# Column-group passes over 32 of a segment's 40 rows for Q and K in a recurrent forward stage, with row-major bf16 stores behind it

## The chip, the cores and the metric

One core of one Trainium2 chip. The metric is the device time of one execution in microseconds (us). Each kernel was executed several times, in rounds with the kernel before on the same chip. The jobs ran on different chips, on which the kernel before took medians of 3449 to 3478 us; kernels of different jobs are therefore compared by their ratios to it, or by stages.

## The reference, cut to what matters

A transformer layer with a recurrent memory, forward and all gradients. The sequence of 2048 tokens is cut into 64 segments of 32. Each segment attends over 40 rows: 8 memory rows and its own 32. The output of the 8 memory rows is the memory of the next segment, so the 64 segments depend on each other. A gated feed-forward block (FFN) follows.

```python
D, H, Dh = 448, 16, 256            # so H*Dh = 4096
M, seg, S, F = 8, 32, 2048, 1792
mem = mem0
for s in range(64):
    h = concat([mem, layernorm(x)[s*32:(s+1)*32]])     # 40 x 448
    q, k, v = h @ Wq, h @ Wk, h @ Wv                   # 40 x 16 x 256 each
    p = softmax(where(mask, q k^T * Dh**-0.5, -1e9))
    o = (p v) @ Wo                                     # 40 x 448
    mem = o[:8];  outs.append(o[8:])
h  = x + concat(outs)
h2 = h + (silu(n(h) @ w_gate) * (n(h) @ w_up)) @ w_down   # n = layernorm
# outputs: h2 and the gradients of x, mem0, Wq, Wk, Wv, Wo, w_gate, w_up, w_down
```

## The kernel before

The program has five stages, one after the other: start-up, the forward recurrence, the FFN (forward and backward of the block), the backward recurrence and the weight gradients (below: the tail). These are the parts that the change and the argument touch. `P` is 128, `KC` is 4 (448 rows in four chunks of 128), `MC` is 32 (4096 columns in chunks of 128), `L` is 40, `cj` is a permutation of the 32 chunks.

```python
# forward, per segment
def wpass(W_sb, s, dst):                       # called for Q and for K: 128 matmuls each
    for j in range(MC):
        c = cj(j); b, jj = divmod(j, 12)
        for kc in range(KC):                   # stationary 128x128 weights, 40 columns stream
            nc.tensor.matmul(pss[b][:, jj*L:(jj+1)*L], lhsT=W_sb[:, kc, c*P:(c+1)*P],
                             rhs=hT_roll[:, kc, sl, :], ...)
    ...                                        # three evacuations to dst, feature-major
# [...]
wpass(Wq_sb, s, qT);  wpass(Wk_sb, s, kT)
# scores: 32 matmuls, stationary 128x64; then V: 32 matmuls, stationary 128x64, 512 columns stream
# [...] softmax of all 8 head pairs, P transposed, 16 matmuls P V -> three PSUM banks
for j in range(MC):                            # memory rows only, through Wo
    nc.tensor.matmul(pO[32*(j%4):32*(j%4)+M, 0:D], lhsT=o8[:, j, :], rhs=Wo_sb[:, cj(j), :], ...)
# [...]
if r == 3:                                     # every 4th segment: 128 own rows through Wo
    for j in range(MC):
        nc.tensor.matmul(px[:, 0:D], lhsT=xblk[:, j, :], rhs=Wo_sb[:, cj(j), :], ...)
    to_token_major(xblk, t)                    # DMA transpose, then 128 x 2048 rows into X_o[t]
# [...] Q and K of the segment are stored feature-major (QT, KT); the backward reads them
#       with one DMA transpose each per segment

# tail, output-projection gradient: 20 row tiles, two halves
def load_x(nm, hf):
    for t in (range(NT) if nm != "o" else order):
        x_t = ring()
        src = dr["X_" + nm][t][:, hf*2048:(hf+1)*2048]      # 128 partitions x 4 KB
        if nm == "o": nc.sync.dma_start(out=x_t, in_=src)
        # [...]
dcs = dr["DHb"].rearrange("(t p) d -> p t d", p=P)[:, :, 0:D]
for t0, t1 in ((0, 4), (4, NT), (NT+1, NB), (NT, NT+1)):    # DHb in four loads
    nc.gpsimd.dma_start(out=DCt[:, t0:t1], in_=dcs[:, t0:t1])
xo = load_x("o", 0)
# six accumulators first: every one of them needs all 20 tiles
rows_by_d(...)
```

## Time and profile before

| stage, from the first and last matmuls of each | us |
|---|---|
| start to the first scores of segment 0 | 75.3 |
| forward, per segment (63 periods) | 17.506 |
| last scores to the first FFN matmul | 75.8 |
| FFN and the set-up of the backward | 367.5 |
| backward recurrence | 1131.3 |
| tail, of it the output-projection part | 711.4, 141.2 |

The median is 3460.1 us (3452.44 to 3460.38, 3 runs). A stage is read as the time between two marks in the trace, each of them the first or last matmul of a certain line. The times of the table all stand on one clock, so only their differences are used.

From the page of the kernel before: totals, three strips of 40 time slices (tenths of busy time, of the granted clock, and of the DMA engines' busy time), and four groups of matmuls (line, engine, operation, names, shapes, count, then busy us and mean ns of one, then idle before them). A copy of a finished PSUM bank to SBUF is called its evacuation; feature-major means features along the partitions, row-major (or token-major) means rows along them. In the names arA, arB and arW are SBUF areas, psf, po, fx and ph are PSUM banks; X_o (after: Os and Or) are the head outputs in DRAM, DHb is the gradient of the rows behind the attention, M_v and X_v are parts of the gradient of V.

```profile
span 3461.7 us, 120955 instructions
...
PE 3042.7 (88%) x55028; PEld 2056.9 (59%) x55038; DVE 1321.4 (38%) x2921; ACT 974.9 (28%) x2181; POOL 620.8 (18%) x1304
...
PE   3999999999999658892999999989999898999999
...
PEclk8999999999999879996999999999999999999999
DMA  7344633543534797799687878787887988888661
...
L360 PE MATMUL psf<-arA,arW 128*128 128x40 bf16 x16384 | 433.6, 181 | 62.0 <-POOL arA L345 35.8
...
L399 PE MATMUL psf<-arW,arA 128*64 128x512 bf16 x2048 | 259.5, 382 | 0.0
...
L462 PE MATMUL fx<-arW,arA 128*128 128x448 bf16 x512 | 124.5, 353 | 0.0
L437 PE MATMUL po<-arW,arB 128*8 128x448 bf16 x2048 | 110.7, 359 | 3.7
...
```

TensorE is busy nearly all the time in the forward stage (slices 2 to 13), at full clock; DMA engines are on average under half busy. The largest group, L360, is `wpass`.

The chain of waits of the kernel before in the forward stage (100 to 1160 us), as shares by engine and line:

```profile
...
by line: PE psf L360 38.2%; PE psf L399 18.4%; PE po L437 9.9%; PE fx L462 9.2%; PE psf L446 4.9%; PE psf L391 3.9%; issue 3.0%; DVE arB L75 2.9%; PE psf L420 2.2%; PE psf L428 1.8%; ACT arB L77 1.2%; DVE om L442 0.6%; DVE arA L449 0.6%; DV
...
```

Nearly all of the chain is TensorE work: Q and K 38%, V (L399) 18%.

The same kernel in windows; the columns are the window, its length, the busy time of five engines with the number of instructions, the granted clock, the DMA share and GB/s:

```profile
...
core 0: us, PE busy (x) PEld busy (x) DVE busy (x) ACT busy (x) POOL busy (x), PEclk, DMA share, GB/s
100.00:1160.00 1060.00, 996.90 (x24443) 772.84 (x24432) 449.03 (x1023) 334.78 (x733) 158.89 (x368) 0.99 0.44 139
1700.00:2700.00 1000.00, 932.77 (x21552) 659.09 (x21553) 461.02 (x1171) 374.89 (x970) 209.56 (x474) 0.98 0.79 165
2745.00:2785.00 40.00, 34.62 (x216) 15.60 (x209) 6.36 (x14) 3.29 (x7) 7.24 (x11) 0.87 1.03 381
...
```

The second row is the backward recurrence, with DMA busy for 0.79; the third is the head of the tail.

One forward segment of the kernel before in the timeline of TensorE (start us, length us, what, how many):

```profile
...
start us, us, engine line op out<-in xcount [idle before <-releaser]
...
500.61 6.56 PE L360 MATMUL psf<-arA,arW 128*128 128x40 bf16 x256
507.10 0.56 PE L391 MATMUL psf<-arA 128*64 128x40 bf16 x24
...
507.90 3.62 PE L399 MATMUL psf<-arW,arA 128*64 128x512 bf16 x30
511.54 0.38 PE L420 MATMUL psf<-ident,arB 128*40 128x40 bf16 x16
...
513.79 1.69 PE L437 MATMUL po<-arW,arB 128*8 128x448 bf16 x32
...
```

Long runs of one kind: 256 matmuls with a stationary operand of 128 columns, then scores and V with 64.

### The profile page before, as it was taken

The numbers are of one execution on the slowest core, as the hardware profiler recorded it, in microseconds if no ns is written. First come the engines' busy times: TensorE is split into PE (matmuls) and PEld (weight loads), VectorE is DVE, ScalarE is ACT, GpSimd is POOL, SyncE is SP. The second block draws the span as 40 slices with busy tenths as digits, with TensorE's granted clock in tenths as the row PEclk, the third lists the DMA queues.
The fourth block names the chain that finished last, engine by engine and source line by source line (L and its number), as shares of the span: only waits on it lengthen the run. The fifth ranks groups of instructions, "written<-read, shape, count | busy, mean of one in ns | idle before, by whom it ended". The sixth has DMA issues, their size and how long they took to land.

```text
span 3461.7 us, 120955 instructions
## 1 busy us (share of the span) xinstructions
PE 3042.7 (88%) x55028; PEld 2056.9 (59%) x55038; DVE 1321.4 (38%) x2921; ACT 974.9 (28%) x2181; POOL 620.8 (18%) x1304
## 2 busy tenths in 40 slices
PE   3999999999999658892999999989999898999999
PEld 2777777777777446661666666666666544444444
DVE  4444444444444246771444444444444301111111
ACT  1333333333333223330333333333333202111100
POOL 3111111111111111111112211211221211111121
PEclk8999999999999879996999999999999999999999
DMA  7344633543534797799687878787887988888661
GB/s 264 132 130 133 174 127 130 162 146 127 156 130 147 134 210 182 178 212 239 139 164 167 174 161 165 166 160 163 172 167 162 275 241 185 174 176 179 160 247 38
DMA packets 997173, 583.91 MB, mean 169 GB/s; under 512 B 906100, under 2 KB 916420, under 8 KB 995060
## 3 DMA queue, kind: packets, MB, share of 16 engines
q1 hardware_dynamic: 926788, 340.27, 47.5%
q0 software_dynamic: 67568, 233.95, 19.8%
q8 instruction: 430, 7.05, 0.9%
q10 hardware_dynamic: 2304, 1.97, 0.2%
q14 instruction: 83, 0.68, 0.1%
HBM read 104.05 MB, written 250.19 MB: 102 GB/s over the span
## 4 chain that ended last, share of the span: by engine, by line
PE 61%; issue 13%; DMA 9%; DVE 8%; SPq 4%; ACT 2%; POOL 2%; ACTq 0%; DVEq 0%; POOLq 0%
PE psf L360 12%; PE po L756 8%; PE psf L399 6%; PE psf L713 5%; PE psf L691 4%; PE po L437 3%; PE fx L462 3%; PE fx L815 3%; PE psf L536 2%; PE psf L921 2%; PE psf L942 2%; PE psf L778 2%; DVE arA L75 2%; PE psf L446 2%; PE fx L602 2%
## 5 line engine op out<-in xcount | busy, mean ns | idle before, releaser
L77 ACT CAST arA<-psf 128x320 bf16<-128x320 f32 (+4 forms) x1139 | 487.9, 447 | 1595.2 <-PE psf L360 422.0
L75 DVE CAST arA<-psf 128x384 bf16<-128x384 f32 (+6 forms) x1029 | 492.5, 496 | 1075.9 <-PE psf L921 359.9
L360 PE MATMUL psf<-arA,arW 128*128 128x40 bf16 x16384 | 433.6, 181 | 62.0 <-POOL arA L345 35.8
L360 PEld LDWEIGHTS <-arW 128*128 128x128 bf16 x16384 | 432.2, 97 | 76.5 <-issue 57.3
L756 PE MATMUL po<-arW,arA 128*32 128x448 bf16 x6144 | 359.2, 365 | 40.5 <-DVE arA L75 21.0
L713 PE MATMUL psf<-arA,arW 128*128 128x40 bf16 x8192 | 219.2, 180 | 55.5 <-POOL arA L648 44.8
L921 PE MATMUL psf<-arW,arA 128*128 128x512 bf16 x990 | 250.7, 381 | 10.3 <-DMA arW<-X_k 5.3
L713 PEld LDWEIGHTS <-arW 128*128 128x128 bf16 x8192 | 214.9, 96 | 75.2 <-issue 74.8
L399 PE MATMUL psf<-arW,arA 128*64 128x512 bf16 x2048 | 259.5, 382 | 0.0
L756 PEld LDWEIGHTS <-arA 128*32 128x32 bf16 x6144 | 156.3, 98 | 160.7 <-issue 32.9
L536 PE MATMUL psf<-arA,arW 128*128 128x256 bf16 x1344 | 163.8, 283 | 94.4 <-DMA arA<-arA 68.7
L921 PEld LDWEIGHTS <-arA 128*128 128x128 bf16 x1440 | 135.2, 98 | 184.7 <-issue 39.2
L536 PEld LDWEIGHTS <-arW 128*128 128x128 bf16 x1344 | 136.3, 102 | 124.3 <-issue 100.4
L399 PEld LDWEIGHTS <-arA 128*64 128x64 bf16 x2048 | 147.3, 111 | 66.5 <-issue 0.2
L75 DVE CAST arB<-psf 40x320 bf16<-40x320 f32 x320 | 108.0, 337 | 98.1 <-PE psf L428 64.7
L77 ACT CAST arB<-psf 128x96 bf16<-128x96 f32 (+1 forms) x320 | 98.3, 307 | 103.5 <-DVE arB L75 51.0
L691 PEld LDWEIGHTS <-arW 128*128 128x128 bf16 x2048 | 88.4, 101 | 65.7 <-issue 62.1
L723 ACT COPY arA<-psf 128x1024 bf16<-128x1024 bf16 x128 | 123.3, 1015 | 4.7 <-PE psf L722 3.1
L462 PE MATMUL fx<-arW,arA 128*128 128x448 bf16 x512 | 124.5, 353 | 0.0
L437 PE MATMUL po<-arW,arB 128*8 128x448 bf16 x2048 | 110.7, 359 | 3.7
L691 PE MATMUL psf<-arB,arW 128*128 128x80 bf16 x2048 | 99.1, 203 | 16.7 <-DVE arB L740 7.7
L942 PE MATMUL psf<-arW 128*128 128x448 bf16 x450 | 95.4, 361 | 5.4 <-DMA arW<-X_o 5.3
(461 smaller groups left out, 3760.6 us busy)
## 6 DMA issues: line engine op xcount, KB each, us to landing
QT<-arA POOLq DMA_DIRECT2D x64, 512.0 KB, 4.0
KT<-arA SPq DMA_DIRECT2D x64, 512.0 KB, 3.5
VG<-arA SPq DMA_DIRECT2D x64, 512.0 KB, 3.1
X_o<-arA POOLq DMA_DIRECT2D x40, 512.0 KB, 4.5
X_v<-arA POOLq DMA_DIRECT2D x32, 512.0 KB, 6.2
X_k<-arA POOLq DMA_DIRECT2D x32, 512.0 KB, 4.2
X_q<-arA POOLq DMA_DIRECT2D x32, 512.0 KB, 4.2
arW<-X_o SPq DMA_DIRECT2D x30, 512.0 KB, 13.9
```

The costliest lines, as they stand in the source:

```text
L75: nc.vector.tensor_copy(out=out, in_=in_)
L77: nc.scalar.copy(out=out, in_=in_)
L360: nc.tensor.matmul(pss[b][:, jj * L:(jj + 1) * L], lhsT=W_sb[:, kc, c * P:(c + 1) * P], rhs=hT_roll[:, kc, sl, :], start=(kc == 0), stop=( ...
L399: nc.tensor.matmul(pV[b][64 * g:64 * g + 64, 0:512], lhsT=hT_flat[:, kc, sl * L:sl * L + 64], rhs=Wv_sb[:, kc, n * 512:(n + 1) * 512], sta ...
L437: nc.tensor.matmul(pO[32 * (j % 4):32 * (j % 4) + M, 0:D], lhsT=o8[:, j, :], rhs=Wo_sb[:, cj(j), :], start=(j < 4), stop=(j >= MC - 4), sk ...
L462: nc.tensor.matmul(px[:, 0:D], lhsT=xblk[:, j, :], rhs=Wo_sb[:, cj(j), :], start=(j == 0), stop=(j == MC - 1))
L536: nc.tensor.matmul(ps[:, f2 * 256:(f2 + 1) * 256], lhsT=Wt[:, kc, c * P:(c + 1) * P], rhs=xT[:, kc, :], start=(kc == 0), stop=(kc == KC - 1))
L691: nc.tensor.matmul(ps[b][:, i * 2 * L:(i + 1) * 2 * L], lhsT=lhs[:, cl, :], rhs=rhs_bd[:, cl // 2, :, :].rearrange("p g n -> p (g n)"), st ...
L713: nc.tensor.matmul(pss[b][:, jj * L:(jj + 1) * L], lhsT=WoT_sb[:, kc, c * P:(c + 1) * P], rhs=do_roll[:, kc, sl, :], start=(kc == 0), stop ...
L756: nc.tensor.matmul(pH[32 * (j % 4):32 * (j % 4) + 32, 0:D], lhsT=blk[nm][:, j, r * SEG:(r + 1) * SEG], rhs=WT[:, cj(j), :], start=(nm == " ...
L921: nc.tensor.matmul(pa[2 * kc + g][:, 0:w], lhsT=lhs_of(b)[:, kc * P:(kc + 1) * P], rhs=rhs_of(b, g), start=(b == 0), stop=(b == nblk - 1), ...
L942: nc.tensor.matmul(pa[i][:, 0:D], lhsT=lhs_of(b, i), rhs=rhs_of(b), start=(bi == 0), stop=(bi == len(nblk) - 1))
```

## The change

The intent: stream the weights instead of the 40 rows. A segment's 40 rows are its 32 own ones and 8 of memory. In the forward, Q and K of 32 of them, the last 24 own rows and the 8 memory rows, come from matmuls with 32 stationary columns and 512 streaming ones; four of them share the array, one in each group of 32 columns (`quad(q)` is the q-th block of 32 output partitions). Q and K of the first 8 own rows, which don't depend on the memory, are made in advance for four segments together ("rest"). What the backward reads of Q, K and the head outputs is stored row-major in bf16, so that it gets Q and K with plain loads. The output projection takes the same 32 rows at once; the extra projection of 128 rows every fourth segment becomes one every sixteenth, for the first 8 own rows of 16 segments.

```diff
+def col_pass(k, ps, W_sb, rows, b):
+    Wv = W_sb.rearrange("p c (g h d n) -> p c g h d n", g=2, h=8, d=2)
+    for kc in range(k.KC):
+        for q in range(4):
+            k.nc.tensor.matmul(ps[quad(q), 0:512], lhsT=rows(kc), rhs=Wv[:, kc, q % 2, 4*b:4*b+4, q // 2, :], ...)
 # per segment
-wpass(Wq_sb, s, qT);  wpass(Wk_sb, s, kT)
-# scores, V, softmax, P, values, one after the other over all heads
+proj(Wk_sb, 0, Kst, "s"); proj(Wq_sb, 0, Qst, "v")     # a proj is a col_pass and its evacuation
+to_features(0)                                         # 8 transposes, one copy
+pS0 = scores(0)
+proj(Wk_sb, 1, Kst, "s"); proj(Wq_sb, 1, Qst, "v")
+softmax(0, pS0)
+to_features(1); pS1 = scores(1)
+for b in range(4): value_rows(b)
+transposed_p(0); softmax(1, pS1); values(0); out_proj(0)
+transposed_p(1); values(1); out_proj(1)
# [... rest(t + 1) every fourth segment; oT, residual, stores of mean and variance to MV ...]
 # stage of the head outputs
-to_token_major(xblk, t)                                # X_o[t]: 128 tokens x 4096
+nc.gpsimd.dma_start(out=dr["Os"][s], in_=stg)          # Os[s]: (d g i) = 128 rows x 1024
 # backward, per segment
-nc.sync.dma_start_transpose(out=Q_sb, in_=dr["QT"][s])
-nc.sync.dma_start_transpose(out=K_sb, in_=dr["KT"][s])
+# [... four plain loads each for Q and K, rows of 2 KB ...]
 # tail
-                nc.sync.dma_start(out=x_t, in_=src)
+                src = dr["Os"][4*t:4*t+4].rearrange("r (d g i) c -> d g r i c", d=2, g=2)
+                for g in range(2):
+                    nc.sync.dma_start(out=x_t[:, g*1024:(g+1)*1024], in_=src[hf, g])
-    # DHb in four loads
+    # DHb in 20 loads, into 8, 24 or 128 partitions each [...]
```

## The prediction

> **What bounds the kernel now.** Table of stages: forward recurrence 83–1175 us, PE busy 94%, clock 0.98, DMA 44%; boundary 1175–1243, PE nearly idle; FFN to 1581; backward set-up to 1644; backward recurrence to 2745, PE 92%, DMA 79%; weight gradients to 3462, PE about 95%. Forward is 64 dependent segments of about 17.0 us, and the chain of waits there is mostly PE: Q/K passes 38%, V 18%, output projection 10%, row residual (fx) 9%, issue 3%. Undisturbed backward segments take 16.04 us, the average is 17.2: about 75 us of stalls over the stage ("issue", DH loads).
>
> **Costs, from trace durations.**
> - Q/K: 256 matmuls of 40 columns take 6.56 us a segment. Afterwards 64 matmuls of 32x512 in four column groups. The four-column-group matmuls of 448 columns in the backward (43 in 2.2 us) run 45 ns apart, so about 53 ns each: 3.4 us. The Trainium skill (TensorE: Matmul & The Clock Gate, Part 3) says column tiles run concurrently; this trace agrees (45 ns against 183 ns alone).
> - Added: 16 transposes (0.97 us in the backward); their two evacuations on DVE at 0.69 us each (128x1024 bf16 from PSUM); mask matmuls 0.15 us.
> - Output projection stays at about 1.7 us; V at 3.5 us.
> - Residual: 32 matmuls per 4 segments (1.55 us a segment) become 0.45 us; but Q/K of memory rows' counterparts ("rest") add about 1.1 us.
> - PE per segment: about 15.9 -> 13.9 us.
> - Chain: K0/Q0, evacuation, transposes, evacuation, scores, softmax in halves, ... , values, projection, one copy of 256 columns instead of two of 224. Adding measured durations gives 14.2–15 us; DVE rises from about 7.2 to 10 us a segment and sits on the chain, so it may queue. V fills the softmax gaps.
> So I expect 15.0 us a segment (14.4 to 16.2), on the critical path nearly in full: 64 x 2.0 = -128 us.
>
> - Backward: two of three DMA transposes a segment become plain 2 KB-row loads, and stores halve. DMA share falls from 0.79 to 0.4–0.5. Q/K loads are off the chain; only the stalls can shrink: -30 us (0 to -60).
> - Boundary: tiny-element load of mean/variance before the FFN, +5 us. Start-up ("rest" of tile 0, more set-up), +4 us.
> - Tail: each 512 KB o tile becomes two loads whose source has an outermost dimension of 4. The Trainium skill (DMA: Bandwidth & Descriptors, "Why a DMA increments its semaphore by 16") says the outermost sizes of both sides fix how many of 16 engines work; that would be 4. No run here shows it. If so, the first weight gradient, already waiting for o tiles (2760–2783), loses perhaps 50 us; even odds: +25 us.
>
> **Prediction.** Sum about -125 us: 3335 us, 80% range 3250 to 3425. Faster by over 2%: 0.76; within 2%: 0.20; slower: 0.04.
>
> **What would show it.** Column passes about 53–55 ns apart, 16 per 0.9 us. Segment period near 15 us; if it is over 16, the chain should show DVE (feature copies, softmax halves) and PE idle above 10%. Backward DMA share below 0.5, average segment under 17 us. PE waits "DMA <- Os" in the tail, and the time to landing of Os loads well above the old 9–14 us, if four engines carry them. No change in FFN body.
>
> **What would make it wrong.** The static instruction order may put evacuations or POOL copies of the memory rows behind late work, or make PE wait for half-softmax twice, lengthening the chain to 17 us; the "rest" work may not fit the gaps; the o loads may cost more than 50 us. On the good side, the chain may drop to the PE sum (13.9 us) and the backward stalls vanish: near 3230 us.

## More of the kernel before

The queue of SyncE in the tail of the kernel before:

```profile
...
2746.41 35.24 SPq L884 DMA_DIRECT2D arW<-X_o  x20
...
```

The queue issues twenty loads of 512 KB in 35.24 us, so 1.76 us each.

## The result, and the profile after

After: 3599.02 us median (3588.35 to 3610.84, 4 runs). Before, in the same rounds: 3460.24 us (3452.44 to 3461.64, 4 runs). The ratio is 1.0396 (95% interval 1.0358 to 1.0433), so the change made the kernel 4% slower; the results are correct. A ratio here is the mean time of one kernel's runs over that of the other's of the same rounds, so not quite the ratio of the medians.

| stage | before | after | difference | predicted |
|---|---|---|---|---|
| start to first scores | 75.3 | 88.5 | +13.2 | +4 |
| forward, 63 periods | 17.506 each | 17.391 each | -7 | -128 |
| last scores to FFN | 75.8 | 88.4 | +12.6 | +5 |
| FFN and set-up | 367.5 | 367.9 | 0 | 0 |
| backward | 1131.3 | 1092.2 | -39 | -30 |
| tail | 711.4 | 866.9 | +155.5 | +25 |
| of it output-projection part | 141.2 | 275.5 | +134.3 | |

The differences sum to +135 us. Two lines make the error: the forward gained almost nothing, and the tail lost six times what was allowed for. Two cautions: the forward is measured here from the first score to the last, over 63; from the start of one segment's scores to the start of the next it is 17.493 and 17.331 us, so -10 us in place of -7. And the stretch from last scores to FFN took 56.6 and 71.7 us in two other kernels with the code of before in this place (before_sw128, before_sw32), so single profiles don't settle its +12.6.

From the page of the kernel after, the answers to the lines of before:

```profile
span 3601.2 us, 106692 instructions
...
PE 3038.5 (84%) x46908; PEld 1831.5 (51%) x46918; DVE 1403.6 (39%) x3384; ACT 1023.4 (28%) x2404; POOL 847.7 (24%) x1789
...
PE   3999999999998188874999999999993198899998
...
PEclk9999999999999699987999999999997599999999
DMA  7334444533533968799555655545556358788661
...
L286 PE MATMUL psf<-arW,arA 128*32 128x512 bf16 x4096 | 302.3, 393 | 46.2 <-POOL arA L387 37.4
L500 PE MATMUL psf<-arW,arA 128*64 128x512 bf16 x2048 | 269.1, 382 | 0.0
...
L492 PE MATMUL po<-arW,arA 128*32 128x192 bf16 (+1 forms) x4096 | 135.9, 260 | 17.1 <-DVE arA L75 17.1
...
L1069 PE MATMUL fx<-arW 128*128 128x448 bf16 x30 | 11.0, 387 | 130.1 <-DMA arW<-Or 116.1
...
```

There is a hole of two slices in the strip of TensorE near the start of the tail; in the second of them the DMA share is 0.3 and the clock 0.5. L286 are the column passes: 302.3 us in place of the 433.6 us of L360 (its matmuls for rest, into fx, not counted). This "busy" counts overlapping matmuls once, and it leaves out the time between two matmuls, which is where the forward's loss turned out to be. L1069 is the output-projection part: TensorE stood idle for 130.1 us in front of its matmuls into fx, all but 14 us of it ended by a load of Or.

The chain of waits after, in the same forward window:

```profile
...
by line: PE psf L286 25.5%; PE psf L500 22.1%; PE po L492 11.4%; PE psf L436 7.6%; PE psf L526 6.2%; PE fx L286 5.1%; PE psf L480 4.1%; ACT arA L77 2.9%; PE psf L447 2.9%; DVE arA L75 2.6%; ACT om L523 2.0%; PE fx L567 1.9%; issue 1.4%; PE 
...
```

Q/K fell from 38% to 25.5% (5.1% more for rest), but V (L500) grew from 18% to 22%, and the transposes L436 came to it (7.6%). L526 is the old L446 (the step to the next memory), grown from 4.9% to 6.2%. The chain is still mostly TensorE.

Windows of the kernel after; the columns are those of before:

```profile
...
100.00:1160.00 1060.00, 992.57 (x16496) 557.61 (x16486) 520.47 (x1449) 381.72 (x940) 357.40 (x793) 0.99 0.42 115
1700.00:2690.00 990.00, 944.34 (x22229) 673.36 (x22228) 474.26 (x1206) 386.09 (x1001) 214.65 (x488) 1.00 0.55 147
...
2745.00:2785.00 40.00, 0.00 (x0) 0.00 (x0) 0.45 (x1) 0.00 (x0) 9.46 (x15) 0.50 0.66 155
2785.00:2835.00 50.00, 0.00 (x0) 0.00 (x0) 0.43 (x1) 1.04 (x1) 0.75 (x1) 0.50 0.29 105
...
```

The backward's DMA share fell from 0.79 to 0.55. In the last two rows TensorE does nothing for 90 us, a part of one wait of 115 us. In the last of them only 105 GB/s move, and the engines' share is 0.29.

The queue of SyncE in that stretch:

```profile
...
2744.96 90.39 SPq L1004 DMA_DIRECT2D arW<-Os  x25
2835.40 4.64 SPq L1000 DMA_DIRECT2D arW<-Or  x4
...
```

The queue issues twenty-five loads of 256 KB in 90.39 us, 3.6 us each: half the bytes of a load of before in twice the time. What TensorE waits for in this time:

```profile
...
2850.53 0.56 PE L1069 MATMUL fx<-arW 128*128 128x448 bf16 x1 [115.34 <-DMA arW<-Or]
...
```

The brackets give the wait before a row and what ended it. The first four Or tiles were loaded and used before 2736 us, so this is an Or tile of the second half. TensorE runs its instructions in the order that the build fixed, and in the kernel after 12 matmuls of the second half (into fx) stand between those of the first half; the first of them waits for a load that stands behind the 25 slow ones. In the kernel before no matmul of the second half stands there.

A forward segment after, in the timeline of TensorE:

```profile
...
504.68 1.91 PE L286 MATMUL psf<-arW,arA 128*32 128x512 bf16 x32
506.53 0.40 PE L436 MATMUL psf<-ident,arA 128*128 128x128 bf16 x4
506.76 0.23 PE L442 MATMUL psf<-arB,ident 128*128 128x160 bf16 x1
506.92 0.61 PE L286 MATMUL psf<-arW,arA 128*32 128x512 bf16 x6
507.46 0.40 PE L436 MATMUL psf<-ident,arA 128*128 128x128 bf16 x4
507.79 1.04 PE L286 MATMUL psf<-arW,arA 128*32 128x512 bf16 x13
508.76 0.38 PE L447 MATMUL psf<-arA 128*40 128x40 bf16 x16
...
512.62 2.33 PE L500 MATMUL psf<-arW,arA 128*64 128x512 bf16 x19
514.57 0.47 PE L468 MATMUL psf<-ident,arA 128*40 128x40 bf16 x8
...
```

The reader is to see the fourth column's short runs: column passes (128*32) are cut by transposes and mask matmuls (128*128) and by scores (128*40). V (L500) runs 19 matmuls for 2.33 us right ahead of the transposes of P (L468); the program wrote them in this order.

### The profile page after: what moved, and what is told of

Its sections match the earlier page's. It is cut to its first block, busy times and chain, and to the rows that moved or that the text cites. A ratio compares the mean times of both kernels' runs of the same rounds, so it can differ in the third digit from the quotient of the medians.

```text
span 3601.2 us, 106692 instructions
## 1 busy us (share of the span) xinstructions
PE 3038.5 (84%) x46908; PEld 1831.5 (51%) x46918; DVE 1403.6 (39%) x3384; ACT 1023.4 (28%) x2404; POOL 847.7 (24%) x1789
## 4 chain that ended last, share of the span: by engine, by line
PE 56%; issue 16%; DMA 12%; DVE 7%; SPq 4%; ACT 3%; POOL 2%; ACTq 0%; POOLq 0%; DVEq 0%
PE psf L286 8%; PE psf L500 7%; PE po L873 6%; PE psf L830 5%; PE po L492 4%; PE psf L808 3%; DVE arA L75 2%; PE fx L932 2%; PE psf L647 2%; PE psf L436 2%; PE psf L1048 2%; PE psf L526 2%; DMA arA<-M_v 2%; DMA arA<-arW 2%; PE fx L286 2%
## 5 line engine op out<-in xcount | busy, mean ns | idle before, releaser
L77 ACT CAST arA<-psf 128x512 bf16<-128x512 f32 (+6 forms) x1395 | 542.1, 408 | 1608.4 <-PE psf L1048 353.0
L75 DVE CAST arA<-psf 128x384 bf16<-128x384 f32 (+3 forms) x1221 | 502.7, 439 | 1076.4 <-PE psf L1048 362.2
L286 PE MATMUL psf<-arW,arA 128*32 128x512 bf16 x4096 | 302.3, 393 | 46.2 <-POOL arA L387 37.4
L500 PE MATMUL psf<-arW,arA 128*64 128x512 bf16 x2048 | 269.1, 382 | 0.0
L830 PE MATMUL psf<-arA,arW 128*128 128x40 bf16 x8192 | 217.7, 180 | 33.4 <-POOL arA L759 27.7
L830 PEld LDWEIGHTS <-arW 128*128 128x128 bf16 x8192 | 213.7, 96 | 52.7 <-issue 52.3
L873 PEld LDWEIGHTS <-arA 128*32 128x32 bf16 x6144 | 153.6, 97 | 152.6 <-issue 36.7
L1048 PEld LDWEIGHTS <-arA 128*128 128x128 bf16 x1440 | 135.6, 98 | 186.2 <-issue 41.4
L647 PEld LDWEIGHTS <-arW 128*128 128x128 bf16 x1344 | 138.4, 103 | 148.7 <-issue 117.8
L286 PEld LDWEIGHTS <-arA 128*32 128x32 bf16 x5120 | 126.5, 97 | 158.6 <-POOL arA L387 37.7
L1069 PEld LDWEIGHTS <-arW 128*128 128x128 bf16 x606 | 59.4, 98 | 189.2 <-DMA arW<-Or 117.0
L500 PEld LDWEIGHTS <-arA 128*64 128x64 bf16 x2048 | 106.9, 109 | 87.0
L492 PE MATMUL po<-arW,arA 128*32 128x192 bf16 (+1 forms) x4096 | 135.9, 260 | 17.1 <-DVE arA L75 17.1
L492 PEld LDWEIGHTS <-arA 128*32 128x32 bf16 x4096 | 100.3, 96 | 42.5 <-DVE arA L75 39.2
L436 PEld LDWEIGHTS <-arA 128*128 128x128 bf16 x1024 | 58.2, 98 | 125.2 <-ACT arA L77 39.8
L1069 PE MATMUL fx<-arW 128*128 128x448 bf16 x30 | 11.0, 387 | 130.1 <-DMA arW<-Or 116.1
L808 PEld LDWEIGHTS <-arW 128*128 128x128 bf16 x2048 | 86.8, 100 | 66.3 <-issue 61.4
L436 PE MATMUL psf<-ident,arA 128*128 128x128 bf16 x1024 | 102.2, 223 | 14.5 <-ACT arA L77 12.6
```

The source lines that it names most:

```text
L75: nc.vector.tensor_copy(out=out, in_=in_)
L77: nc.scalar.copy(out=out, in_=in_)
L286: k.nc.tensor.matmul(ps[quad(q), 0:512], lhsT=rows(kc), rhs=Wv[:, kc, q % 2, 4 * b:4 * b + 4, q // 2, :], start=(kc == 0), stop=(kc == k.K ...
L436: nc.tensor.transpose(ph[:, (i * HB + h) * P:(i * HB + h + 1) * P], st[:, (HB * b + h) * P:(HB * b + h + 1) * P], ident[:, :])
L492: nc.tensor.matmul(pO[quad(2 * dh + jh), 0:w], lhsT=o32[:, j, :], rhs=Wo_sb[:, cj(j), 256 * dh:256 * dh + w], start=(j < 2), stop=(j >= MC ...
L500: nc.tensor.matmul(pV[64 * g:64 * g + 64, 0:512], lhsT=hT_flat[:, kc, sl * L:sl * L + 64], rhs=Wv_sb[:, kc, n * 512:(n + 1) * 512], start= ...
```

## The experiments

Theory E says that the tail's loads run on 4 of the 16 DMA engines, because the outermost dimension of their source is 4. Theory S says that changes of the stationary width (32, 64, 128 columns; below: switches) cost TensorE time in the forward. A rival for the forward, L, says that V stands ahead of P on the chain. For the tail the rivals were the smaller size of the loads and of their packets, and the 20 loads of DHb.

TensorE's occupancy of a segment is worked out from the trace: the intervals between the starts of consecutive matmuls are summed, and what an interval has over its streaming time plus an allowance of 100 ns is taken as waiting. The streaming time is taken as 0.417 ns a column, from the traces: in a row, 128-column transposes start 56 ns apart and 448-column matmuls 189 ns. The allowance is as long because an interval at a switch has up to 99 ns more than its streaming time, as is shown below. This gives 15.96 us a segment before and 15.82 us after; the prediction had 15.9 and 13.9. With an allowance of 120 ns it is 16.12 and 15.95; with one well under 100 ns, switches would be counted as waiting. Switches are counted in the same list: 4.0 a segment before, 18.8 after.

### tail_rows: the same Os bytes, with 32 rows outermost

```diff
-src = dr["Os"][4*t:4*t+4].rearrange("r (d g i) c -> d g r i c", d=2, g=2)
-for g in range(2):
-    nc.sync.dma_start(out=x_t[:, g*1024:(g+1)*1024], in_=src[hf, g])
+for r in range(4):
+    src = dr["Os"][4*t + r].rearrange("(d g i) c -> d i g c", d=2, g=2)
+    nc.sync.dma_start(out=x_t[32*r:32*r+32, :].rearrange("p (g c) -> p g c", g=2), in_=src[hf])
```

> The changed kernel; only the loads of the o tiles differ: four loads of 32 rows each (outermost size 32 on both sides) instead of two of 128 rows whose source has outermost size 4. Same bytes, same 2 KB rows, same results. Theory E (the old form works with 4 of 16 DMA engines): the tail falls from 875 us to 715-740 us, the whole to 3440-3465 us; 4-byte completion packets on the SP queue rise from 4 to 16 a load. Rival O (the new order of tiles, the 20 small DHb loads or the 2 KB rows cost the time): the tail stays above 820 us, the whole above 3540 us, since there are even more loads.

Correct, 3496.97 us (3490.73 to 3505.61), ratio to before 1.014 (1.011 to 1.0171); before in the same rounds 3449.36 us. The output-projection part took 192.9 us (after: 275.5; before: 141.2). So 83 of the 134 us go back with the shape of the loads changed, and about 52 us stay. The whole tail (782.9 us) and the whole time lie outside the ranges of both theories. One more thing changed with the edit: with another number of loads, TensorE's fixed order came out differently, without matmuls of the second half between the first half's, but with transposes of M_v there. So this run alone doesn't separate the engines from the order; tail_flat does.

### tail_pair and tail_flat: outermost 2, and outermost 128

```diff
 # tail_pair, correct: each of the two loads split in halves of two segments
+    for a in range(2):
+        nc.sync.dma_start(out=x_t[64*a:64*a+64, g*1024:(g+1)*1024], in_=src[hf, g][2*a:2*a+2])
 # tail_flat, wrong on purpose: the same bytes from 128 rows in a row
+    nc.sync.dma_start(out=x_t[:, g*1024:(g+1)*1024], in_=dr["Os"][4*t + 2*hf + g])
```

> The changed kernel with o tiles loaded by four loads of 64 rows, source outermost size 2: as many loads, and as large, as tail_rows. Theory E: 2 engines work, a 128 KB load occupies them about 3.5 us, so the o part grows from 275 us to 400-520 us. Rival (the number of loads or their size matters, not the outermost size): near tail_rows' 193 us.

> The changed kernel, o tiles loaded by two loads of 128 rows as it does, but from 128 rows that lie together, so the source's outermost size is 128 and not 4 (wrong rows, so a wrong gradient of Wo, on purpose). Number and size of the loads and the 2 KB rows are the same. Theory E: o part falls from 275 us to 180-200 us like tail_rows, 16 completion packets a load. Rival (number of loads or row size): stays above 250 us.

One run each, state unknown. tail_pair: 3749.67 us, output-projection part 415.2 us. tail_flat: 3500.54 us, part 180.2 us; its results are wrong. Both keep the packets of 2048 bytes. Between after and tail_flat, SyncE's queue and TensorE's order in this part are the same in the traces, load by load and matmul by matmul; only the outermost dimension differs (4, 128), and the part falls by 95 us. Between tail_pair (2) and tail_rows (32) it falls by 222 us, with the same number and size of loads, though in tail_pair M_v comes last. The DMA view of the kernel after (2790 to 2830 us) and of tail_pair (2850 to 2890 us), where almost nothing but Os loads runs; each digit is the busy share of the 16 engines in tenths, and the second line is the hardware queue's packets, MB and share:

```profile
...
DMA  5222222222222222222222222222222222222222
...
q1 hardware_dynamic: 1886, 3.74, 25.2%
...
```

```profile
...
DMA  1111111111111111111111111111111111111111
...
q1 hardware_dynamic: 987, 1.96, 13.1%
...
```

A share of 25.2% of 16 engines is 4.0 engines; 13.1% is 2.1. The first window moved 3.74 MB in 40 us (94 GB/s), the second 1.96 MB (49 GB/s). Half the outermost dimension, half the engines, half the rate. A load of the kernel after also leaves 4 of the 4-byte packets that signal completion, a load of before 16. E is shown, over outermost sizes of 2, 4, 32 and 128; the size of the packets isn't the cause, since tail_flat has the same packets and reaches 410 GB/s with all loads together. In tail_flat TensorE still waits 44.3 us for the Or tile of the second half, and 39 us of the part stay; what the fixed order alone costs was not measured.

### tail_dhb4: DHb in four large loads again

```diff
 # on top of tail_rows; wrong on purpose (rows in the old order)
-    # 20 loads of DHb
+for t0, t1 in ((NT//2, NT), (0, NT//2), (NT+1, NB), (NT, NT+1)):
+    nc.gpsimd.dma_start(out=DCt[:, t0:t1], in_=dcs[:, t0:t1])
```

> tail_rows with the gradient rows for the first weight gradient read by 4 large loads, as the kernel before does, in place of 20 small ones (their order of rows is then wrong, and so is the gradient of Wo, on purpose). tail_rows still spends 193 us between the end of the backward chain and the V gradient, against 141 us before. If the 20 loads (issue on the queue of POOL, about 10 us to landing) hold PE: that part falls to 140-165 us, whole -25 to -50 us. If the o loads themselves or the M_v loads hold it: it stays above 180 us.

Wrong results. 3488.35 us (3476.26 to 3491.97), ratio 1.0049 (0.9989 to 1.0109); the output-projection part 186.2 us, against 192.9 in tail_rows. The 20 loads are worth about 7 us there (TensorE's order differs a little too), not the 52 us that stayed.

### v_late: half of V behind the first transposes of P

```diff
 # on top of tail_rows
-for b in range(4): value_rows(b)
-transposed_p(0); softmax(1, pS1); values(0); out_proj(0)
+value_rows(0); value_rows(1)
+transposed_p(0); softmax(1, pS1)
+value_rows(2); values(0); value_rows(3); out_proj(0)
```

> tail_rows plus one reordering in the forward: the last two V groups are traced behind the transposes of the first half of P, so that half 0 can go on while V still runs. Work and number of tiling switches stay. Theory L (the forward is held by the serial tail behind V: P waits behind V on PE): the period of 17.2 us falls by 0.8-1.5 us, the whole by 50-100 us against tail_rows. Theory S (PE is held by drains at switches of column tiling, about 18 a segment): period within 0.3 us of tail_rows.

Correct, 3474.08 us (3461.17 to 3480.64), ratio 1.0065 (1.0026 to 1.0105). The forward period is 17.195 us, against 17.315 in tail_rows: -0.12 us. L falls as the main cause of the missing 2 us. The whole time is 23 us shorter than tail_rows, of which the forward explains 8; the rest of it lies in the tail, which the edit doesn't touch (758.3 against 782.9 us in the profiled runs). So differences of 25 us in the tail of single profiles prove nothing; the output-projection part is steadier (192.9, 194.1 and 197.3 us in three kernels with the same tail code).

### before_sw32 and before_sw128: the price of a switch by itself

```diff
 # in the kernel before, in wpass: six matmuls of 8 columns more per segment
+if j in (7, 15, 23):
+    nc.tensor.matmul(pss[2][0:32, 400:408], lhsT=W_sb[:, 0, 0:32], rhs=hT_roll[:, 0, sl, 0:8], ...)
 # before_sw128: the same with [0:128] and 0:128
```

> The kernel before with six dummy matmuls of 8 columns added per segment inside the Q/K passes, each on a 32-column stationary: 12 more switches of column tiling per segment. If a switch costs about 96 ns as the gaps in the traces suggest: +1.15 to 1.35 us a segment, whole +75 to +90 us. If the gaps are only how the profile models ends: within 20 us of before.

> Control of before_sw32: the same six dummy matmuls a segment with a 128-column stationary, no switch. Both theories: +0.1 to 0.3 us a segment, whole +5 to +20 us.

Both correct. before_sw32: 3529.02 us (3522.05 to 3542.39), ratio 1.0236 (1.02 to 1.0272). before_sw128: 3470.58 us (3462.0 to 3482.07), ratio 1.0064 (1.0031 to 1.0097). That is +80 and +21 us, the first inside its range, the second 1 us above it. The two kernels differ only in the width of the six stationary operands. In before_sw32 each stands alone in a run of 128-wide ones and makes two switches, 12 a segment. The forward periods are 18.662 and 17.756 us; the difference of 0.906 us over 12 is 75.5 ns for a switch. The whole times differ by 58.4 us, which over 64 x 12 switches gives 76 ns. In the kernel after, the intervals at switches exceed the streaming time by 95 to 99 ns for each of the four kinds (32 to 128 and back, 64 to 128 and back), and by -1 to 3 ns where the width stays (512-column V, the transposes and P V).

### grouped: the same work, with fewer and longer runs

```diff
 # on top of tail_rows: each block is made to issue behind the last matmul of the block before
+blk(projs)                        # all four proj in a row
+blk(lambda: value_rows(0)); blk(feats)          # all transposes and mask matmuls
+pS0 = blk(lambda: scores(0)); softmax(0, pS0)
+blk(lambda: value_rows(1)); pS1 = blk(lambda: scores(1))
+blk(lambda: value_rows(2)); blk(lambda: transposed_p(0)); softmax(1, pS1)
+blk(lambda: value_rows(3)); blk(lambda: values(0)); blk(lambda: transposed_p(1)); blk(lambda: values(1))
+out_proj(0); blk(lambda: out_proj(1))
```

> tail_rows (mended o loads) with the forward's PE order forced into blocks: all four Q/K passes, then V, then all feature transposes, then scores, V, and so on. Same matmuls; switches of column tiling fall from 18.7 to about 12 a segment, and the passes are no longer cut in mid-quad. Theory S (switches and cut quads fill PE): PE occupied per segment falls from 15.7 to about 14.6 us, the period from 17.2 to 15.9-16.4 us, whole -50 to -85 us against tail_rows. Rival L (dependencies set the period): occupied falls but the period stays above 16.9 us, PE idle grows instead.

Correct, 3410.16 us (3408.03 to 3413.36), ratio 0.9821 (0.9772 to 0.987); before in the same rounds 3464.04 us. The forward period is 15.950 us (tail_rows: 17.315). Occupancy is 14.80 us (tail_rows: 15.78), with 13.6 switches, more than the 12 expected. The period lies in the range of S and outside that of L. The timeline of TensorE of grouped near the start of a segment:

```profile
...
499.81 2.33 PE L286 MATMUL psf<-arW,arA 128*32 128x512 bf16 x40
502.08 1.05 PE L505 MATMUL psf<-arW,arA 128*64 128x512 bf16 x8
503.06 1.07 PE L436 MATMUL psf<-ident,arA 128*128 128x128 bf16 x16
503.97 0.30 PE L444 MATMUL psf<-arB,ident 128*128 128x160 bf16 x2
504.56 0.38 PE L452 MATMUL psf<-arA 128*40 128x40 bf16 x16 [0.29 <-DVE arA L438]
...
```

The first row is the end of a run of 64, cut by the window: forty column matmuls in 2.33 us, 58 ns each, where the kernel after had runs of 6 and 13 and 69 ns a matmul on average. S is shown for its direction and for the greater part of its size. 5.2 fewer switches at 75 to 99 ns are 0.4 to 0.5 us. Without the switch at its end, a column matmul took 62.6 ns in the kernel after and 56.2 ns in grouped: a run that isn't a multiple of four leaves groups of four incomplete (read from the run lengths; no run tests it by itself). Over 79 column matmuls that is 0.5 us. Together this is an estimate of 0.9 to 1.0 us, and the occupancy fell by 1.0 us from the kernel after. The period fell by 1.37 us; so nearly 0.4 us of it is less waiting in the new order, which no run separates from the rest.

### grouped_mlate and grouped_dhact: what is left in the tail

Even in grouped the output-projection part takes 197.3 us, 56 more than before. TensorE's instruction order is fixed at build time, and in it the transposes of M_v tiles stand between the matmuls of this part, ahead of their data. From the timeline of TensorE in grouped:

```profile
...
2662.36 2.03 PE L1097 MATMUL psf<-arW,arA 128*128 128x448 bf16 x5 [22.99 <-DMA arW<-DHb]
...
2675.24 0.35 PE L1097 MATMUL fx<-arW 128*128 128x448 bf16 x1
2688.70 1.03 PE L1050 MATMUL ph<-ident,arA 128*128 128x128 bf16 x8 [13.11 <-DVE arA L1044]
...
```

```diff
 # grouped_mlate, on top of grouped
-nxt = load_m("v", 0)
+nxt = load_m("v", 0, last_o)      # its first transpose issues behind the last matmul of the part
 # grouped_dhact, on top of grouped_mlate: the 20 loads of DHb
-nc.gpsimd.dma_start(out=DCt[...], in_=...)
+nc.scalar.dma_start(out=DCt[...], in_=...)
```

> The grouped kernel with one ordering edge more: the transposes of the M_v rows come behind the last matmul of the output-projection part, on TensorE. In grouped that part took 197.3 us (before: 141.2) and its chain shows two waits in the middle, 13.1 us and 8.4 us, where TensorE's fixed order puts transposes of M_v tiles that have not been loaded ahead of matmuls whose data is there. Theory M (those waits, and the low clock after them, are about 25 us of the 56 us that are left): the output-projection part 165 to 178 us, whole 3380 to 3395 us, ratio to before 0.972 to 0.980. Rival D (the part is bound by the bytes that the loads move, and TensorE would wait for them in another place): part 190 to 200 us, whole 3405 to 3415 us.

> grouped_mlate with its 20 loads of DHb issued from ScalarE's queue in place of the GpSimd queue. In grouped TensorE waited 23.0 us for the first of them, and the GpSimd queue had two stores of the backward stage between them, which held it for 9.0 and 4.3 us. Theory Q (the order in the GpSimd queue makes this wait): first wait 10 to 14 us, output-projection part 8 to 13 us shorter than in grouped_mlate, whole 3370 to 3385 us. Rival D (the loads' bytes, or the end of the backward stage's last store): first wait 20 to 24 us, whole within 4 us of grouped_mlate.

Both correct. grouped_mlate: 3400.78 us (3390.26 to 3406.53), ratio 0.9818 (0.9778 to 0.9857); before in the same rounds 3466.04 us. The output-projection part fell to 171.1 us, inside the range of theory M, so the misplaced transposes cost 26 us of it. The whole time is outside both ranges. It fell by 9 us against grouped only, in another job, and its ratio is the same; the backward of the profiled run was 9 us longer, for no reason that the edit gives. grouped_dhact: 3387.86 us (3383.55 to 3398.7), ratio 0.9793 (0.9747 to 0.9838). In grouped_mlate the first wait is 20.1 us, and the trace charges it to Os, no longer to DHb; in grouped_dhact it is 6.8 us and for another engine, but waits of 3.1, 4.5, 3.4 and 1.7 us follow, three of them for Os, and the part is 166.9 us, 4 us less instead of 8 to 13. The whole time lies 3 us outside the range of theory Q and far outside that of its rival, and 5 us of the difference are the backward again. Q is at best half right: the wait went away, and a part of it came back as waits for the next tiles.

### grouped_tiles: head outputs laid out for the load

```diff
 # on top of grouped_dhact
-nc.gpsimd.dma_start(out=dr["Os"][s], in_=stg)
+for a in range(4):
+    nc.gpsimd.dma_start(out=dr["Os"][4*t + a][32*r:32*r+32, :], in_=stg[32*a:32*a+32, :])
-    # four loads of 32 rows
+    nc.sync.dma_start(out=x_t.rearrange("p (g c) -> p g c", g=2),
+                      in_=dr["Os"][4*t + 2*hf:4*t + 2*hf + 2].rearrange("g p c -> p g c"))
```

> grouped_dhact with the head outputs laid out for the load: each segment stores its 128 rows in four pieces of 32 rows, so that one tile half is two blocks of 128 rows of 2 KB, and one load of 512 KB over 128 partitions takes the place of the four loads of 128 KB over 32 partitions. In the kernels with four loads all 16 engines are busy, but a 2048-byte packet takes about 145 ns (tail_rows, grouped_mlate), against about 85 ns where the load spans 128 partitions (after, tail_flat), and TensorE still waits for Os in three or four places (10 us in grouped_dhact). Theory R (the slow packets of the narrow loads are what is left of the output-projection part): packets 80 to 110 ns, part 150 to 159 us instead of 166.9, whole 3370 to 3382 us. Rival D (what is left is the bytes of all loads together, or half clock after idle): part 163 to 170 us, whole within 5 us of 3388. Against both: three more stores a segment in the GpSimd queue could lengthen the forward period from 15.95 us; up to 16.05 is expected.

Correct, 3438.23 us (3425.14 to 3447.83, 6 runs), ratio 0.9886 (0.9849 to 0.9923); before in the same rounds 3478.24 us (11 runs). A miss on nearly every count. The packets of 2048 bytes did become faster (median 86 ns over all Os loads, against 135 ns in grouped_dhact and 138 ns in tail_rows), but the output-projection part took 179.9 us, with one wait of 15.2 us for an Or tile in place of the small ones for Os. Neither theory's range has this. The run isn't clean either: with fewer loads, TensorE's fixed order again has matmuls of the second half between those of the first, as in the kernel after and not in grouped_dhact, and it is one of these that waits the 15.2 us. The forward period rose to 16.346 us, and 5.2% of its chain in the forward are now waits for DMA transposes within the core, the kind that brings head outputs to row-major (before: too few to be among the lines of the chain shown above). So R is neither shown nor refuted: what the narrow loads cost stays open, and three more stores a segment are not free.

## Why the prediction was wrong, point by point

- **What bounds the kernel.** Right: the chain in the forward was mostly TensorE work, and it stayed so.
- **Forward, 17.0 to 15.0 us a segment, -128 us.** Wrong, -7 us. The step that failed is "PE per segment: about 15.9 -> 13.9 us": after, TensorE was occupied for 15.8 us. The prediction priced each matmul from undisturbed runs (about 53 ns) and summed, without a price for changing from one stationary width to another. The change interleaves 32-, 64- and 128-wide work: 18.8 switches a segment instead of 4.0. At 75 to 99 ns the 14.8 extra switches are 1.1 to 1.5 us, and cut-off groups of four add about 0.7 us: 79 column matmuls at 62.6 ns instead of 53, the switches not counted. Together these estimates from the measured prices are 1.8 to 2.2 us, and the sum was short by 1.9 us. The Trainium skill, page "TensorEngine Tiling (Array Packing)", section Key Properties, says it: "Changing tiling mode (not just tile) drains the TensorE". The trace agrees, and gives the number that the page lacks. The prediction drew on the page on concurrency alone.
- **Concurrency of column groups.** What the prediction cited from the Trainium skill, page "TensorE: Matmul & The Clock Gate" (Part 3) held: 40 column matmuls of 512 columns take 2.33 us in grouped, 58 ns each. The mechanism was right; the run length wasn't. (The prediction's 183 ns for a matmul alone is a little low: 448-column matmuls in a row start 189 ns apart in this trace.)
- **"V fills the softmax gaps".** The risk was named ("the static instruction order may ..."), and V did land ahead of P, but moving it gained 0.12 us. The failure was not here.
- **Backward, -30 us; DMA share 0.4 to 0.5.** Right: -39 us, the share 0.55, a little above the range. That the loads were the cause of the stalls was not tested by a run of its own.
- **Boundary +5, start-up +4.** Misses by 8 and 9 us: +12.6 and +13.2. The first is smaller than the spread between kernels with the same code there (56.6 to 75.8 us). In the boundary the stores of MV (mean and variance) and Hh (the rows behind the attention) stand in the GpSimd queue behind stores that wait for DMA transposes; this is read from the trace and no run tests it.
- **Tail, "perhaps 50 us; even odds: +25 us".** The mechanism was right, its size wrong: +155.5 us, of which the first part of the tail has 134.3 us. The mis-sized term is the cost of a load on four engines. 256 KB took 3.6 us. The first six accumulators need every tile of the first half, and in TensorE's fixed order there was even a matmul of the second half ahead of most of them; it stood still for 115 us; the prediction didn't have this order. The Trainium skill, page "DMA: Bandwidth & Descriptors", section "Why a DMA increments its semaphore by 16 and not by 1", gives the rule (the largest number up to 16 that divides the slowest dimension of both sides). With 4 the trace shows 4.0 engines, with 2 it shows 2.1. A rule that a page states, and that fits the diff, should not have been entered at even odds. tail_flat, with the same order of loads and matmuls, gives 95 us back, tail_rows 83 us. In the kernels with the mend of tail_rows the transposes of M_v, ordered too early, account for 26 us more (grouped_mlate).
- **The odds.** The sum was -125 us. With 64 x 1.1 to 1.5 us for the switches, and 134 us in place of 25 for the tail's first part, it would have been a loss of 55 to 80 us: an estimate from the measured prices, and the right sign.

What stays open: about 26 us of the output-projection part in the best kernel (166.9 against 141.2 us), what the narrow loads and what the second half's early matmuls cost, the exact split of grouped's gain, and the start-up and the boundary.

The best kernel is grouped_dhact, at 0.9793 of before (0.9747 to 0.9838; 3387.86 us): it is faster, by about 2%, once its loads use all engines and its matmuls run in longer runs of one width. Whether by more than 2% the interval leaves open.

## What to carry to other kernels

Price a TensorE plan by its runs, not by its matmuls: count the changes of stationary width in the order that is really issued, and add the price of each (75 to 99 ns here). For every DMA, read the outermost dimension on both sides before anything else, since it can cost a factor of four with the same bytes. After a change of layout look at the one place that has to wait for all its data at once, here the first accumulators of the tail; there a slow load has nothing to hide behind. And when an experiment changes the number of loads, compare the order of TensorE's instructions too: here it moved with them.

## What the Trainium skill lacked or had wrong

- "TensorEngine Tiling (Array Packing)", Key Properties: it says that changing the tiling mode drains the engine, but gives no cost. Here a switch costs 75.5 ns (difference of two kernels, 12 switches a segment), and the intervals at switches are 95 to 99 ns over streaming time; where the width stays it is -1 to 3 ns.
- "TensorE: Matmul & The Clock Gate", Part 3: it gives the gain of column groups, but no figure for runs of them that other widths cut. Here 40 in a row took 58 ns each, and 69 ns on average where they were cut, into runs of 6, 13 and 32 most often.
- "DMA: Bandwidth & Descriptors", the section on the semaphore: the rule for the number of engines held (4.0 and 2.1 engines busy for 4 and 2). Nothing to correct; with it went 94 GB/s on four engines (256 KB in 3.6 us) and 49 GB/s on two engines.
